# Block-sparse attention and a two-layer MLP on one core: the first weight load moved to the front, a small table moved to GpSimd, and a new order of work

## The chip, the core and the metric

The kernel runs on one core of a Trainium2 chip. Its engines are TensorE (PE: matmuls, with a weight load PEld of its own), VectorE (DVE), ScalarE (ACT), GpSimd (POOL) and SyncE (SP), which here only issues DMA transfers. Each engine works off its own instructions strictly in the order of the program and waits at semaphores for the others; 16 DMA engines move the data. The metric is the time of one execution on the device in microseconds (us), as the median of several runs. The time before is 715.46 us.

## The reference

Two stages. Attention over 4 batches of 8 heads, 768 positions and a head width of 64, with a mask by blocks of 32 positions, and then an MLP over the 3072 x 512 result:

```python
scores = scale * np.matmul(q, k.transpose(0, 1, 3, 2))
mask = np.abs(blk_i - blk_j) <= 1
mask = mask | (blk_i == 0) | (blk_j == 0) | (blk_i == n_blocks - 1) | (blk_j == n_blocks - 1)
for qb in range(n_blocks):
    for kb in sampled_blocks[qb]:           # three sampled blocks for each of the 24
        mask[qb*block:(qb+1)*block, kb*block:(kb+1)*block] = True
scores = np.where(mask, scores, -1000000000.0)
attn = softmax(scores)                      # rows
x = np.matmul(attn, v)                      # -> (3072, 512)
h = x @ w_in                                # 512 x 2048
g = h * np.tanh(softplus(h))
out = g @ w_out                             # 2048 x 512
```

The two weights arrive as 64-bit floats; the other inputs are 32-bit floats, and the sampled blocks are 64-bit integers.

## The kernel before

**Stages.** A block of 32 queries sees its three neighbours, the first and the last block and three sampled ones, eight blocks of keys in all. Queries are worked on two blocks at a time (a *job*, `attend`): scores `s`, row maximum `mx` (VectorE), its negative `nb`, exponentials `pt` (ScalarE), transposes `t` on TensorE and their copies `pp`, the product with v `o`, then on VectorE the normalisation `r`, `xs` (L968 to L983) and a block transpose `tx` (L1001), and a split of the result into two 16-bit parts `xh` and `xl`. The first and the last block of a batch are jobs of their own that see all keys (*dense*). A batch has 13 jobs. Batch 0 is computed in 32 bits (`exact`), the others with split 16-bit parts.

The MLP runs on 256 tokens at a time: `h` (L1206), twelve matmuls for each of 16 column groups, an elementwise chain `hs`, `us`, `g`, and `y` (L1267). The first 256 tokens are blocks 0 to 7 of batch 0; they come from jobs 0 to 4, and job 4 (blocks 7 and 8) is the last that they need.

**Keys and values of the sampled blocks.** Keys are copied from `kt` into the gather buffers `kg` by GpSimd or ScalarE (L691, L693), with offsets read from a table `offk`. Values are gathered by DMA from a padded copy `vd` of v in memory into `vg` (L721 to L727), with row numbers from a table `offv`. Both tables are 72 numbers on one partition, made once at the start by `which` (L362 to L404) from the sampled blocks: duplicates, neighbours and border blocks are sent to a row of zeros.

**Weights.** A weight is 64 bits wide in memory. `w_in` is loaded in eight pieces of 1 MB (`wr`, three buffers, L1051), `w_out` in sixteen pieces of 0.5 MB (`wor`, in the six buffers of the tag `raw`). VectorE unpacks each to 32 bits by three instructions (L1059, L1062, L1065). TensorE then forms weight norms from them (`gram_wi`, `gram_wo`, L468), from which power-of-two scales are made (`rootp`, L494, and `root`, L499 to L352), and ScalarE, VectorE and GpSimd split the scaled weight into two 16-bit parts (`wi t`, `wi hi`, `wi lo` at L1113 to L1124; `wo` at L1156 to L1165).

**What sets the order.** Every step is entered as a task with engines, a modelled duration and what it reads and writes (`Plan.add`). `Plan.emit` goes through them with a clock of its own and gives each engine, in turn, the task that can start first; where several could, the one with the smallest ready time plus an offset from the table `PRIO` (`K(name, n)`). Some tasks may run on one of two or three engines, and the clock chooses. `START` holds the earliest start of the first 18 jobs, in the planner's time. MLP matmuls fill TensorE's queue between attention steps. Where the planner sees TensorE idle in the first 150 us it writes matmuls on zeros in the gap (`zeros`, L1038), whose result nothing uses. DMA transfers of SP are issued in the order of the plan as well; one that waits for a buffer holds those behind it.

## Time and profile before

| | |
|---|---|
| median of 3 runs | 715.46 us (714.55 to 717.31) |
| the profiled execution | 717.17 us |
| its span, first to last instruction | 715.4 us |
| TensorE busy | 679.7 us, 95% |
| VectorE busy | 579.3 us, 81% |
| ScalarE busy | 530.6 us, 74% |
| GpSimd busy | 259.6 us, 36% |
| mean granted TensorE clock | 0.986 |

All rows below come from this one execution. A line such as `L1065` is a line of the kernel before. "Busy" counts the time in which at least one instruction of the engine runs. A row of a timeline gives start, length, engine, line, what is written and read, and in brackets how long the engine stood idle before it and what ended that.

### The profile page before, as it was taken

To read this page: it belongs to the slowest core of one execution; us is meant where nothing else is said; L and a number is where in the kernel's file an instruction comes from. 1 tells how busy PE (TensorE), PEld (TensorE's weight loads), DVE (VectorE), ACT (ScalarE), POOL (GpSimd) and SP (SyncE) were. 2 spreads that over 40 slices of the span, in tenths; PEclk is the share of its full clock that TensorE was granted. 3 is DMA by queue.
4 is the path that set the end of the run, shared out by engine and by line. 5 is a ranking of instruction groups with operands and counts; after the bars stand their busy time and mean duration, and the time that the engine had idled before them with its cause. 6 is when DMAs were issued, how large, how long until landed. Compare 5 with 4: busy or idle time off the path is not lost.

```text
span 715.4 us, 25363 instructions
## 1 busy us (share of the span) xinstructions
PE 679.7 (95%) x10349; PEld 451.6 (63%) x10349; DVE 579.3 (81%) x1083; ACT 530.6 (74%) x874; POOL 259.6 (36%) x326
## 2 busy tenths in 40 slices
...
GB/s 333 383 220 252 269 299 97 124 166 99 173 169 131 199 212 131 163 255 148 143 146 191 137 206 137 245 189 132 162 132 131 134 133 158 131 76 16 16 16 29
DMA packets 144600, 115.94 MB, mean 162 GB/s; under 512 B 96739, under 2 KB 107492, under 8 KB 144484
## 3 DMA queue, kind: packets, MB, share of 16 engines
q1 hardware_dynamic: 144480, 114.33, 60.8%
...
q10 hardware_dynamic: 4, 0.00, 0.0%
...
## 4 chain that ended last, share of the span: by engine, by line
PE 55%; DVE 25%; ACT 7%; DMA 6%; issue 4%; SPq 1%; POOL 1%; ACTq 0%; POOLq 0%; DVEq 0%
PE y L1267 25%; PE h L1206 22%; PE o L947 3%; PE s L777 3%; DVE mx L820 3%; DMA vg<-vd 2%; ACT pt L846 2%; DVE p L897 2%; DVE wi L1065 2%; DMA wr<-in_moe_w_in_dram 1%; DVE wi L1062 1%; DVE tx L1001 1%; DVE hs L1240 1%; DVE nb L835 1%; DVE xs L978 1%
## 5 line engine op out<-in xcount | busy, mean ns | idle before, releaser
L1206 PE MATMUL h<-xh,wi 128*128 128x256 f16 x1536 | 283.1, 273 | 0.0
L1267 PE MATMUL y<-wo,g 128*128 128x512 f16 x1152 | 277.6, 379 | 1.0 <-ACT ys L1278 0.5
L1206 PEld LDWEIGHTS <-wi 128*128 128x128 f16 x2304 | 222.4, 98 | 58.7 <-issue 4.6
L1206 PE MATMUL h<-xl,wi 128*128 128x256 f16 x768 | 209.8, 273 | 0.0
L1267 PEld LDWEIGHTS <-g 128*128 128x128 f16 x1152 | 109.0, 98 | 104.8 <-issue 5.6
L846 ACT ACTIVATE pt<-s,nb,ns 128x256 f32<-128x256 f32 (+1 forms) x208 | 106.4, 577 | 8.2 <-DVE nb L835 7.3
L691 POOL COPY kg<-kt 128x256 f16 (+1 forms) x147 | 77.3, 564 | 75.0 <-PE s L777 54.8
L1215 ACT ACTIVATE hs<-h 128x512 f32<-128x512 f32 x96 | 56.7, 590 | 60.0 <-PE h L1206 59.8
L1240 DVE SCALAR_TENSOR_TENSOR hs<-us,hs 128x1024 f32<-128x1024 f32 x48 | 64.2, 1337 | 28.0 <-ACT us L1239 28.0
L1021 POOL CAST xh<-tx 128x256 f16<-128x256 f32 (+1 forms) x40 | 28.7, 726 | 121.2 <-DVE tx L1001 120.4
L897 DVE SCALAR_TENSOR_TENSOR p<-pt,p 128x512 f16<-128x512 f32 (+1 forms) x102 | 63.6, 643 | 0.8 <-ACT p L890 0.4
L1230 ACT ACTIVATE us<-hs,hsc 128x1024 f32<-128x1024 f32 x48 | 55.2, 1150 | 1.1
L1234 DVE TENSOR_SCALAR us<-us 128x1024 f32<-128x1024 f32 x48 | 34.1, 711 | 26.8 <-ACT us L1230 26.4
L820 DVE TENSOR_REDUCE mx<-s 128x4 f32<-128x1024 f32 x44 | 53.3, 1212 | 3.0 <-PE s L777 2.2
L1251 POOL TENSOR_TENSOR g<-hs,g 128x1024 f16<-128x1024 f32 x18 | 42.4, 2353 | 34.8 <-DVE g L1248 26.0
L1024 POOL TENSOR_TENSOR xl<-tx,xh 128x256 f16<-128x256 f32 (+1 forms) x45 | 37.5, 838 | 41.7 <-ACT xh L1019 25.8
L1238 ACT ACTIVATE us<-us 128x1024 f32<-128x1024 f32 x48 | 50.7, 1057 | 2.3 <-POOL us L1236 1.3
L1237 ACT ACTIVATE us<-us 128x1024 f32<-128x1024 f32 x38 | 40.1, 1055 | 15.7 <-DVE us L1234 15.6
L1239 ACT ACTIVATE us<-us 128x1024 f32<-128x1024 f32 x48 | 50.7, 1057 | 0.8
L693 ACT ACTIVATE kg<-kt 128x256 f16 (+1 forms) x117 | 36.7, 379 | 13.5 <-DMA kt<-in_k_dram 5.4
L947 PEld LDWEIGHTS <-pp 128*32 128x32 f16 x2952 | 32.5, 97 | 11.9 <-issue 11.4
L1253 DVE TENSOR_TENSOR g<-hs,g 128x1024 f16<-128x1024 f32 x30 | 37.4, 1248 | 2.0 <-ACT g L1246 1.6
...
## 6 DMA issues: line engine op xcount, KB each, us to landing
...
```

The lines of the kernel that those rows point to most:

```text
L691: nc.gpsimd.tensor_copy(out=dst, in_=src)
L820: nc.vector.tensor_reduce(out=mx.rearrange("p g w -> p (g w)"), in_=tl[ks].rearrange("p g (w k) -> p (g w) k", k=KT), axis=AX.X, op=ALU.max)
L846: ex = lambda o, x, g, w: nc.scalar.activation(out=o, in_=x, func=AF.Exp, bias=nb[:, g, w:w + 1], scale=ns(w)[:, 0:1])
L897: nc.vector.scalar_tensor_tensor(out=x[:, 1, cs], in0=src, scalar=PSC, in1=x[:, 0, cs], op0=ALU.mult, op1=ALU.subtract)
L947: nc.tensor.matmul(o[cs, at] if v1 == VW else o[cs, at, 0:v1 - v0], p[:, k, g, cs], x, start=j == 0 and g == 0 and k == 0 and n == 0, stop ...
L1206: nc.tensor.matmul(h[:, f2].rearrange("p (s q) -> p s q", q=BS), wi[:, fp, w, cc, fs], x[:, :, cc], start=f2 == 0 and k == 0, stop=f2 == 1 ...
L1215: nc.scalar.activation(out=tl[kq][:, 2 * (fp % 2):2 * (fp % 2) + 2], in_=tl[kh], func=AF.Copy, scale=-2.0 * GSC)
L1230: nc.scalar.activation(out=us(), in_=hs(), func=AF.Exp, scale=hsc[:, b, k:k + 1])
L1238: add("ACT", 0.97, lambda: nc.scalar.activation(out=us(), in_=us(), func=AF.Ln, bias=1.0), w=[ku], key=K("ln", b))
L1239: add("ACT", 0.97, lambda: nc.scalar.activation(out=us(), in_=us(), func=AF.Exp, scale=-1.0), w=[ku], key=K("un", b))
L1240: add("DVE", 1.15, lambda: nc.vector.scalar_tensor_tensor(out=hs(), in0=us(), scalar=-0.5, in1=hs(), op0=ALU.add, op1=ALU.mult), r=[ku], w ...
L1267: nc.tensor.matmul(tl[ky], tl["g", b, t, k][:, g, f, q], wo[:, fc, w], start=fc == 0 and n == 0, stop=fc == NFC - 1 and n == 2)
```

## The change

Three things. The load of the first piece of `w_in` (`load wr` 0) is the first transfer that SP issues; before, the first piece came sixth, behind k, q and v, and it was piece 3. The table of row numbers is taken out of `which` into a task `table` of its own on GpSimd; the not-equal test is written there as a difference or an equality, compared with zero again, which makes 23 instructions of 20, and the rows of zeros are cleared before the loads instead of after the table. And the numbers that set the order (`PRIO`, `START`, `RES`) are all new.

```diff
 PRIO = {
-    "load wr": (163.9, 188, 32.3, -243.6, 177.7, 103.9, 211.3, 300.2),
+    "load wr": (-961.5, -388, 51.1, -141.9, 314.6, 167.6, 315, 492.8),
+    "table": (-1252,),
...
     def which(new):
         room = new(sb, "hs", ("z",), [P, 4, TT]).rearrange("p c t -> p (c t)")
+        tl["z"] = room[0:BS, 0:H * VW // 2]
+        nc.gpsimd.memset(tl["z"], 0.0)
...
         nc.scalar.dma_start(out=kq, in_=blocks[0:1])
+        tl["kq"] = kq, sbi, mk
+
+    def table():
+        kq, sbi, mk = tl["kq"]
         qb = mk(NB)
-        nc.vector.tensor_copy(out=qb.rearrange("p (c g) -> p c g", g=GPC), in_=kq[:, :, 0:GPC])
+        nc.gpsimd.tensor_copy(out=qb.rearrange("p (c g) -> p c g", g=GPC), in_=kq[:, :, 0:GPC])
...
-        nc.vector.tensor_tensor(out=ar, in0=ar, in1=ar, op=ALU.mult)
-        nc.vector.tensor_scalar(out=ar, in0=ar, scalar1=1.5, scalar2=None, op0=ALU.is_gt)
+        nc.gpsimd.tensor_tensor(out=ar, in0=ar, in1=ar, op=ALU.mult)
+        nc.gpsimd.tensor_scalar(out=ar, in0=ar, scalar1=1.5, scalar2=None, op0=ALU.is_gt)
         for j in (0, NB - 1):
-            nc.vector.tensor_scalar(out=nq, in0=rb, scalar1=float(j), scalar2=None, op0=ALU.not_equal)
-            nc.vector.tensor_tensor(out=ar, in0=ar, in1=nq, op=ALU.mult)
+            nc.gpsimd.tensor_scalar(out=nq, in0=rb, scalar1=float(j), scalar2=0.0, op0=ALU.is_equal, op1=ALU.is_equal)
+            nc.gpsimd.tensor_tensor(out=ar, in0=ar, in1=nq, op=ALU.mult)
...
-    add("ACT", 1.0, lambda: which(new), w=["off", "z"],
-        new=[("hs", ("z",))], key=K("which", 0), lat=5.2, kind=("dma", 0.0, 2))
+    add("ACT", 1.0, lambda: which(new), w=["kq", "z"],
+        new=[("hs", ("z",))], key=K("which", 0), lat=3.6, kind=("dma", 0.0, 2))
+    add("POOL", 6.0, table, r=["kq"], w=["off"], use=[("z",)], key=K("table", 0))
...
-    RES, START = 949.9, [53.9, 10.3, 0, 62.9, 42.9, 3.5, 60.8, 74.5, 31.2, 92.3, 3.1, 0, 64.4, 30.3, 104.4, 183, 166.3, 159.2]
+    RES, START = 2183, [1, 0, 36, 10.2, 0, 5.1, 56.9, 31.3, 89.8, 28.4, 117.5, 0, 0, 122, 149.1, 139.3, 196.9, 34.9]
```

The sync queue (SP) at the start of the program, before; `wr` is a piece of `w_in`, `kt`, `q` and `raw_v` are the loads of k, q and v of batch 0, `vd` is the padded copy of v:

```order
L519 DMA kt_124<-in_k_dram 128x4x768
L519 DMA q_0_154<-in_q_dram 128x4x256
L537 DMA raw_v_0_158<-in_v_dram 128x2x512
L519 DMA q_1_160<-in_q_dram 128x4x256
L537 DMA raw_v_1_162<-in_v_dram 128x2x512
L1051 DMA wr_164<-in_moe_w_in_dram 128x4x512
L537 DMA raw_v_2_166<-in_v_dram 128x2x512
L407 DMA vd_63<-z 32x1040
L1051 DMA wr_191<-in_moe_w_in_dram 128x4x512
```

And now, at the same place:

```order
L1057 DMA wr_124<-in_moe_w_in_dram 128x4x512
L525 DMA kt_134<-in_k_dram 128x4x768
L525 DMA q_0_138<-in_q_dram 128x4x256
L543 DMA raw_v_0_140<-in_v_dram 128x2x512
L1057 DMA wr_142<-in_moe_w_in_dram 128x4x512
L543 DMA raw_v_1_144<-in_v_dram 128x2x512
L1057 DMA wr_146<-in_moe_w_in_dram 128x4x512
L413 DMA vd_63<-z 32x1040
```

Three pieces of the weight stand among the first seven transfers instead of one; the second load of q has moved behind the fourth piece.

VectorE around the first unpacking, before; `offv` is the last row of the table, `mx` the maximum of the dense job 0 and then of job 1:

```order
L400 TENSOR_TENSOR z<-z 1x72
L401 TENSOR_SCALAR offv<-z 1x72
L635 COPY v_0_150<-raw_v_0_158 128x16x64
L815 TENSOR_REDUCE mx_240<-s_214 128x2
L817 TENSOR_REDUCE mx_240<-s_0_0_223 128x1
L817 TENSOR_REDUCE mx_240<-s_0_1_224 128x1
L818 TENSOR_TENSOR mx_240<-mx_240 128x2
L1059 TENSOR_SCALAR wi<-wr_164 128x1024
L1062 SCALAR_TENSOR_TENSOR wi<-wr_164,wi 128x1024
L1065 SCALAR_TENSOR_TENSOR wi<-wr_164,wi 128x1024
L820 TENSOR_REDUCE mx_344<-s_284 128x4
```

And now, from the engine's first instruction:

```order
L1065 TENSOR_SCALAR wi<-wr_124 128x1024
L1068 SCALAR_TENSOR_TENSOR wi<-wr_124,wi 128x1024
L1071 SCALAR_TENSOR_TENSOR wi<-wr_124,wi 128x1024
L641 COPY v_0_130<-raw_v_0_140 128x16x64
L821 TENSOR_REDUCE mx_261<-s_224 128x2
L823 TENSOR_REDUCE mx_261<-s_0_0_233 128x1
L823 TENSOR_REDUCE mx_261<-s_0_1_234 128x1
L824 TENSOR_TENSOR mx_261<-mx_261 128x2
L1065 TENSOR_SCALAR wi<-wr_142 128x1024
L1068 SCALAR_TENSOR_TENSOR wi<-wr_142,wi 128x1024
L1071 SCALAR_TENSOR_TENSOR wi<-wr_142,wi 128x1024
L826 TENSOR_REDUCE mx_360<-s_301 128x4
```

The table has left VectorE, one unpacking stands in front of everything, and a second one is done by the maximum of job 1.

VectorE ahead of the normalisation of job 4, before (`o_1296` is that job's output, `wor` a piece of `w_out`, `iv_i` and `ws` the scale of a quarter of `w_in`, `gsc` made of all four):

```order
L1062 SCALAR_TENSOR_TENSOR wo<-wor_1262,wo 128x512
L499 TENSOR_SCALAR iv_i<-tp_w_1227 128x1
L502 TENSOR_SCALAR iv_i<-iv_i 128x1
L352 TENSOR_SCALAR ws_1426<-iv_i 128x1
L1065 SCALAR_TENSOR_TENSOR wo<-wor_1262,wo 128x512
L1062 SCALAR_TENSOR_TENSOR wo<-wor_1005,wo 128x512
L1180 TENSOR_SCALAR hsc<-iv_i,iv_x 128x1
L1065 SCALAR_TENSOR_TENSOR wo<-wor_1005,wo 128x512
L1171 TENSOR_REDUCE gmx<-iv_i 128x1
L1173 RECIPROCAL rg<-gmx 128x1
L1174 TENSOR_SCALAR gsc<-iv_i,rg 128x4
L968 TENSOR_SCALAR r_1467<-o_1296,iv_r 128x4
```

And now, where job 4's output is `o_1435` and job 3's `o_1309`:

```order
L1068 SCALAR_TENSOR_TENSOR wo<-wor_1326,wo 128x512
L974 TENSOR_SCALAR r_1425<-o_1309,iv_r 128x4
L978 RECIPROCAL r_1425<-r_1425 128x4
L989 TENSOR_TENSOR xs_1428<-o_1309,r_1425 128x256
L1071 SCALAR_TENSOR_TENSOR wo<-wor_1326,wo 128x512
L1007 STREAM_TRANSPOSE tx_1454<-xs_1428 128x256
L826 TENSOR_REDUCE mx_1462<-s_1237 128x4
L885 COPY pp_1_1501<-t_1_1392 128x512
L974 TENSOR_SCALAR r_1512<-o_1435,iv_r 128x4
L978 RECIPROCAL r_1512<-r_1512 128x4
L989 TENSOR_TENSOR xs_1515<-o_1435,r_1512 128x256
L505 TENSOR_SCALAR iv_i<-tp_w_1506 128x1
```

Before, eight pieces of `w_out` are unpacked and all four scales of `w_in` made ahead of that row; now fourteen pieces are unpacked ahead of it (the last is `wor_1326`), and two of the four scales follow behind it.

## Rows read from the trace of the kernel before

**Rows 1.** The page: busy time, share of the span and instructions of each engine.

```profile
PE 679.7 (95%) x10349; PEld 451.6 (63%) x10349; DVE 579.3 (81%) x1083; ACT 530.6 (74%) x874; POOL 259.6 (36%) x326
```

**Rows 2.** Stretches: length, busy (instructions) of PE, PEld, DVE, ACT, POOL; clock, DMA, GB/s.

```profile
0.00:89.76 89.76, 71.52 (x1241) 42.19 (x1241) 76.55 (x139) 50.88 (x104) 46.03 (x63) 0.92 0.91 291
89.76:160.00 70.24, 63.71 (x1087) 48.21 (x1080) 67.52 (x119) 58.31 (x93) 41.99 (x49) 0.95 0.62 174
160.00:700.00 540.00, 533.31 (x7996) 356.36 (x7978) 435.21 (x827) 420.05 (x676) 171.57 (x216) 1.00 0.59 143
```

**Rows 3.** The same for the filler line L1038 alone (PE and PEld busy).

```profile
0.00:89.76 89.76, 32.36 (x119) 11.81 (x119) 0.92 0.91 291
```

**Rows 4.** Timeline of TensorE: the dense scores, and around the first MLP matmul.

```profile
9.00 1.52 PE L767 MATMUL s<-kt,q 64*32 64x512 f32 x32 [1.57 <-DMA q<-in_q_dram]
...
79.44 0.55 PE L931 MATMUL o<-vg,pp 128*32 128x65 f32 x24 [1.36 <-DMA vg<-vd]
79.93 0.40 PE L468 MATMUL gram_wo<-wo 128*128 128x128 bf16 x4
80.17 1.31 PE L1038 MATMUL zeros<-z 128*128 128x512 f16 x3
...
89.76 0.28 PE L1206 MATMUL h<-xh,wi 128*128 128x256 f16 x1
```

**Rows 5.** Timeline of VectorE, from the last piece of the first weight on.

```profile
57.23 3.04 DVE L1065 SCALAR_TENSOR_TENSOR wi<-wr,wi 128x1024 int32<-128x1024 int32 x1
...
83.08 0.21 DVE L968 TENSOR_SCALAR r<-o,iv_r 128x4 f32<-128x4 f32 x1
...
83.88 1.21 DVE L820 TENSOR_REDUCE mx<-s 128x4 f32<-128x1024 f32 x1
...
92.14 0.68 DVE L1065 SCALAR_TENSOR_TENSOR wo<-wor,wo 128x512 int32<-128x512 int32 x1
92.74 0.68 DVE L1062 SCALAR_TENSOR_TENSOR wo<-wor,wo 128x512 int32<-128x512 int32 x1
93.34 0.41 DVE L1059 TENSOR_SCALAR wo<-wor 128x512 int32<-128x512 int32 x1
```

**Rows 6.** Timeline of VectorE at the start: table, copy of v, first unpacking.

```profile
5.31 0.17 DVE L380 COPY z<-z 1x24 f32<-1x24 f32 x1 [5.31 <-DMA z<-in_blocks_dram]
...
9.64 0.18 DVE L401 TENSOR_SCALAR offv<-z 1x72 int32<-1x72 f32 x1
10.25 0.69 DVE L635 COPY v<-raw_v 128x1024 f32<-128x1024 f32 x1 [0.42 <-DMA raw_v<-in_v_dram]
...
15.55 0.69 DVE L1059 TENSOR_SCALAR wi<-wr 128x1024 int32<-128x1024 int32 x1 [2.62 <-DMA wr<-in_moe_w_in_dram]
...
17.58 1.23 DVE L1065 SCALAR_TENSOR_TENSOR wi<-wr,wi 128x1024 int32<-128x1024 int32 x1
```

**Rows 7.** Timeline of GpSimd: copies from k, a small and a long subtraction.

```profile
7.42 0.74 POOL L653 COPY kg<-kt 128x256 f32<-128x256 f32 x2 [5.18 <-DMA kt<-in_k_dram]
8.54 0.77 POOL L691 COPY kg<-kt 128x128 f32 x3 [0.38 <-issue]
...
16.63 3.27 POOL L691 COPY kg<-kt 128x128 f32 x6 [2.48 <-ACT pt L846]
...
29.31 0.43 POOL L1024 TENSOR_TENSOR xl<-tx,xh 128x128 f16<-128x128 f32 x1
...
56.08 3.12 POOL L1123 TENSOR_TENSOR wi<-wt_i,wi 128x1024 f16<-128x1024 f32 x1
```

**Rows 8.** Timeline of the sync queue: the issues of k and the first weight piece.

```profile
0.75 0.46 SPq L519 DMA_DIRECT2D kt<-in_k_dram  x1
...
4.82 0.68 SPq L1051 DMA_DIRECT2D wr<-in_moe_w_in_dram  x1
```

**Rows 9.** Waits of TensorE from 90 us on: total us, times, longest.

```profile
PE gram_wo L468 <- DVE wo L1065: 2.4, 3, 1.2
```

**Rows 10.** Waits of the sync queue up to 60 us: total us, times, longest.

```profile
SPq L1051 <- DVE wi L1065: 5.8, 4, 2.5
```

161 lines of the change are left out of this document (80 added, 81 removed), and 30 rows, old and new, of the table PRIO.

## The prediction

> **What bounds the kernel now.** I read the busy shares of the page first: TensorE is busy 679.7 of 715.4 us [rows 1]. The number flatters, because a part of that is no work. The table by stretches [rows 2] and the same table for the filler line alone [rows 3] split the span at 89.76 us, where the first matmul of the MLP starts [rows 4]. Up to there TensorE is busy 71.5 us, of which 32.4 us are 119 filler matmuls on zeros (0.272 us each). So the first 89.76 us hold 39.1 us of real work and 18.2 + 32.4 = 50.6 us that give nothing. Behind it TensorE loses 6.5 us up to 160 and 6.7 us up to 700; the 4.2 us that are left of the span are its tail. Check: 679.7 - 32.4 = 647.3 us of real work, and 647.3 + 50.6 + 6.5 + 6.7 + 4.2 = 715.3. The order of work does not touch the 647.3; the change can win or lose only in the four losses, and the first is the large one. It is set by one event: when the output of attention job 4 (blocks 7 and 8, the last that the first 256 tokens need) is normalised, transposed and split, since the first MLP matmul reads it.
>
> What holds that event is read in two views. VectorE is busy 76.6 of these 89.8 us [rows 2], and 5.3 + 0.4 + 2.6 of the 13.2 it lacks lie before the first unpacking at 15.55 [rows 6]; from there on it works off a queue whose bulk is the unpacking of the weights, and comes to the normalisation of job 4 (L968) at 83.08 [rows 5]. The DMA engines are busy 91% of the same stretch [rows 2], and the last gather of job 4 lands only at 79.44, with TensorE waiting 1.36 us for it [rows 4]. Two limits lie close together, VectorE the later one.
>
> **The change, part by part.** *The table.* 20 VectorE instructions from 5.31 to 9.82 go (4.5 us) [rows 6]. They lie where VectorE had only loads to wait for: the copy of v at 10.25 and the first weight piece at 15.55 both come on a DMA. Taken out alone they are worth nothing there; the stretch is only free for something else. On GpSimd 23 instructions take their place. The trace of before has no such small arithmetic on GpSimd; the nearest row is a 128x128 subtraction of 0.43 us [rows 7], and the lower end is VectorE's own pitch of 0.23. That makes 5.3 to 9.9 us. While VectorE unpacked, GpSimd's copies took 3.27 us for six against 0.77 for three, twice as long [rows 7], and the first unpacking will run just then, so I take 8 us, from 5.3 to 13.3. The first copies from k into the gather buffers follow (0.74 and 0.77 us [rows 7]) and are wanted when the scores of job 1 start, behind the exponentials of job 0, by my estimate near 18 us. The cover is some 3 us; beyond it each us of the table delays job 1.
> The Trainium skill (GPSIMD Engine Reference, section Key points) says that VectorE is about twice as fast for elementwise work; twice the 4.5 us would be 9 us, inside the bounds and hidden as well.
>
> *The first piece in front.* Before, k (1.57 MB) is issued at 0.75 and the first weight piece (1.05 MB) at 4.82 [rows 8]; the copies that need k start at 7.42 [rows 7] and the unpacking at 15.55 [rows 6]. From the one landing to the other came the piece and 2.1 MB of q and v, 3.1 MB in 8.1 us or 0.39 MB/us. The piece at the head then lands 1.3 us before k did, near 6, and k, q and v come 2.7 us later: the dense scores of job 0 start near 11.7 instead of 9.00 [rows 4]. VectorE unpacks the piece (15.55 to 18.81, 3.2 us [rows 6]) in the hole that the table left, so at 15.5 us it is 3.2 us ahead. The pieces share three buffers, so the next loads are issued earlier too. What attention loses is 2.7 us at its start; the same VectorE queue takes it in.
>
> *The order.* In front of job 4's normalisation stand 14 pieces of the second weight, unpacked, against 8. A piece is three instructions with steps of 0.60, 0.60 and at most 0.41 us [rows 5]: 1.6 us, so +9.6; one more maximum, +1.2 [rows 5]; one small subtraction, +0.2. Behind it went two roots of weight scales with what hangs on them and the three steps up to gsc, thirteen tiny instructions at VectorE's pitch of about 0.2: -2.6. The splitting of the first weight's rear half stands behind too, so GpSimd has 4 of its long subtractions in front instead of 7. Each holds VectorE: L1065 took 3.04 us while one ran from 56.08 to 59.20, against 1.23 [rows 5 to 7]. Three fewer are worth 3 x 1.8 = 5.4 at most and nothing at least; I take 3.5. With the 3.2 us in hand: 9.6 + 1.2 + 0.2 - 2.6 - 3.5 - 3.2 = +1.7, so VectorE comes to job 4 at 84.8 (82.9 to 88.3).
> The DMA limit: in front of job 4's last gather the sync queue now has 6 more pieces of 0.52 MB and one gather fewer (0.46 MB), 2.7 MB, 7.0 us at 0.39. The 9% that DMA stood free up to 79.4, 7 us, can take all of it or none: landing at 79.4 to 86.4, plus 0.7 for the matmuls. I take 85 for the normalisation, VectorE being the later one again.
> From there to the first MLP matmul it was 6.7 us, with a maximum of 1.2 in between and two subtractions on VectorE. Now come the normalisation and one root (six tiny instructions, 1.4), the transpose (0.6), and casts on ScalarE and subtractions on GpSimd (two each of at most 0.43 [rows 7]): 3.7 in all. First MLP matmul at 88.7 (86.6 to 93). Before it TensorE has done one job's P.V less (two of 0.55 x 32/24 = 0.73 us) and 40 of the weight-norm matmuls more (four start 0.24 us ahead of the next row [rows 4]: 2.4), 0.9 us net. The first loss is thus 88.7 - 40.0 = 48.7, **1.9 us less**. The program carries 111 fillers instead of 119, 8 x 0.272 = 2.2 us; that is no proof, since TensorE may idle where no filler stands.
> Behind 88.7: TensorE waited 2.4 us for unpacked pieces of the second weight [rows 9]; 14 of 16 are now done by then. **-2** (0 to -2.4). From 160 on the order is set anew but of the same kind: as many changes between attention and MLP (213 in either program), and of the 39 score groups no two closer than before. Its 6.7 us of loss can become 3 to 10; I take **0**.
> Sum: -1.9 - 2 = -3.9. The profiled execution took 717.17 us for its span of 715.4; the sum gives 713.3 for one like it. The median of the runs is 715.46, 1.7 below it, and so I forecast **711.5**.
>
> **The rivals.**
> *Loads first, gathers late (slower).* The gathers of jobs 3 and 4 stand on the sync queue behind six loads in a row, which wait for buffers; up to 60 us the queue already waits 5.8 us in four such places, 2.5 the longest [rows 10]. If DMA does not run denser than its 291 GB/s [rows 2], 2.7 MB cost 9.3 us: the gather lands at 88.7, the first MLP matmul comes at 88.7 + 0.7 + 3.7 = 93.1, the loss is 53.1, +2.5; with one more such wait of 2.5 us ahead of each of the two jobs +7.5, less the 2: 721. It decides from a first MLP matmul later than about 95. For it: DMA 91% busy. Against: the free 9% were waits for buffers, and these now turn earlier.
> *Nothing is won (same).* The earlier unpacking only moves VectorE's idle time, because attention starts 2.7 us late and the table stretches beside it: VectorE comes to job 4 at 84.8 + 2.7, the MLP at 91.2, loss 51.2, 0.6 more, and half of the 2 us behind it comes: 715.1.
> *The late losses go too (much faster).* If the new order also halves the 6.5 and 6.7 us, another 4 to 5 us: 707. Nothing in the rows speaks for it but that they are waits, not work.
> *GpSimd stops at an operation that is new to it.* Its first subtraction in the trace (29.31) starts in a row of work and takes 0.43 us [rows 7], so the rows speak against it. As a mechanism of this kernel: a table 6 us longer ends at 19.3, the copies for job 1 at 20.8, some 3 us past the cover: 714.5.
> The Trainium skill (GPSIMD Engine Reference, section Instruction dispatch) has such a stop of about 6 us, for the first call of a freshly loaded kernel, without a row of its own in a profile; by that this rival holds, by the rows it does not.
>
> **How the numbers follow.** About 0.5% (3.6 us) is what can be told from no change, so 711.9 is the border. Forecast 0.50, its own range 707 to 715, with 0.30 of it under the border and 0.20 over; late gathers 0.17; nothing won 0.15; late losses gone 0.13; GpSimd's stop 0.05. Faster 0.30 + 0.13 = 0.43; same 0.20 + 0.15 + 0.03 = 0.38; slower 0.17 + 0.02 = 0.19. The range leaves half of the late gathers and a part of the late losses outside: 704.5 to 719.5.
>
> **What would show it.** Right: the first unpacking starts near 6 us and the dense scores near 11.7; the table's 23 rows end before 15; VectorE is at job 4's normalisation near 85, behind 14 pieces; the first MLP matmul comes at 87 to 90, with TensorE's busy time less fillers near 40 us by then; no waits for unpacking behind it; a loss from 160 to 700 of 3 to 10 us. Wrong: a first MLP matmul past 92, TensorE waiting for the gathers of jobs 3 and 4 in rows of 2 us and more, the scores of job 1 waiting for the copies from k, or a loss from 160 on that differs by over 4 us, which would say that the order and not the start decides.

## The result, and the profile after

The changed kernel takes **724.83 us** (median of 4 runs, 724.24 to 725.85) against 715.0 us of the kernel before on the same chip: 1.0134 times the time, 95% interval 1.0107 to 1.0162. It is slower by some 9.8 us where 4 us less were forecast, and lies outside the range. The profiled execution took 725.06 us for a span of 723.3; that of the kernel before (717.17 us, span 715.4) lay above its median, so the two spans differ by 7.9 us only. Line numbers behind line 409 are 6 higher than before.

The table by stretches, which answers to [rows 2], now split at 93.0 where the MLP starts; the columns are the stretch, its length, the busy time of PE, PEld, DVE, ACT and POOL with instructions, PEclk, DMA share and GB/s:

```profile
0.00:93.00 93.00, 72.17 (x1210) 44.04 (x1211) 75.08 (x131) 44.20 (x101) 41.03 (x75) 0.89 0.90 301
93.00:160.00 67.00, 58.03 (x1002) 44.08 (x999) 59.08 (x100) 58.40 (x95) 47.34 (x45) 0.92 0.48 132
160.00:700.00 540.00, 530.96 (x8046) 355.70 (x8045) 437.50 (x840) 419.59 (x670) 175.75 (x226) 1.00 0.61 145
```

And the filler line alone in the first stretch (PE, PEld, PEclk, DMA share, GB/s), which answers to [rows 3]:

```profile
0.00:93.00 93.00, 29.23 (x111) 10.67 (x111) 0.89 0.90 301
```

The reader is to take four numbers out of these for each kernel: when the MLP starts, what real work is left for TensorE from there on, what it loses up to 160 and up to 700, and the tail. Their sum is the span.

| | before | after | forecast |
|---|---|---|---|
| first MLP matmul | 89.76 | 93.0 | 88.7 |
| real work behind it | 608.2 | 608.3 | 607.3 |
| loss up to 160 | 6.5 | 9.0 | 4.5 |
| loss from 160 to 700 | 6.7 | 9.0 | 6.7 |
| tail | 4.2 | 4.0 | 4.2 |
| span | 715.4 | 723.3 | 711.4 |

The 7.9 us of span are 3.2 of a later start of the MLP, 2.5 behind it and 2.3 from 160 on. Against the forecast the span is 11.9 us longer: 4.3 by the start of the MLP, 4.5 behind it, 2.3 from 160 on and 1.0 of real work. The first loss as the prediction counted it (idle and fillers ahead of the MLP) is 50.1 instead of 50.6, so by that number nothing is lost there. That number misleads: TensorE's real work ahead of the MLP has grown from 39.2 to 42.9 us. Of that 0.9 had been forecast, as matmuls that the new order moves ahead; the rest goes with the granted clock of the stretch, 0.89 instead of 0.92. The clock's lower level is half the upper, so 0.11 of 93 us are 20.5 us at the lower level, where before had 14.

The start, on VectorE, answers to [rows 6] (start, length, line, what is done, and the idle time before it):

```profile
9.74 0.70 DVE L1065 TENSOR_SCALAR wi<-wr 128x1024 int32<-128x1024 int32 x1 [9.74 <-DMA wr<-in_moe_w_in_dram]
10.47 1.22 DVE L1068 SCALAR_TENSOR_TENSOR wi<-wr,wi 128x1024 int32<-128x1024 int32 x1
11.73 1.23 DVE L1071 SCALAR_TENSOR_TENSOR wi<-wr,wi 128x1024 int32<-128x1024 int32 x1
16.32 0.69 DVE L641 COPY v<-raw_v 128x1024 f32<-128x1024 f32 x1 [3.36 <-DMA raw_v<-in_v_dram]
17.33 1.23 DVE L821 TENSOR_REDUCE mx<-s 128x2 f32<-128x1024 f32 x1 [0.31 <-PE s L773]
...
23.41 1.23 DVE L826 TENSOR_REDUCE mx<-s 128x4 f32<-128x1024 f32 x1 [0.15 <-PE s L773]
...
89.50 0.21 DVE L974 TENSOR_SCALAR r<-o,iv_r 128x4 f32<-128x4 f32 x1
```

VectorE stands idle for 9.74 us until the piece at the head has landed, and comes to the first maximum at 17.33. Before, it came to it at 10.86:

```profile
10.86 1.22 DVE L815 TENSOR_REDUCE mx<-s 128x2 f32<-128x1024 f32 x1
```

On TensorE, in the same time and behind the first MLP matmul, which answers to [rows 4]:

```profile
13.02 1.03 PE L474 MATMUL gram_wi<-wi 128*128 128x128 bf16 x8 [5.90 <-DVE wi L1071]
...
15.26 2.76 PE L773 MATMUL s<-kt,q 64*32 64x512 f32 x32
...
92.97 0.27 PE L1212 MATMUL h<-xh,wi 128*128 128x256 f16 x1
...
98.98 0.87 PE L937 MATMUL o<-vg,pp 128*32 128x65 f32 x32 [3.23 <-DMA vg<-vd]
...
133.34 0.67 PE L937 MATMUL o<-vg,pp 128*32 128x65 f32 x32 [3.25 <-issue]
```

The dense scores start at 15.26, 6.3 us later than before, and run for 2.76 us instead of 1.52: TensorE has been idle for 5.9 us and is at the lower clock level. The last two rows are the larger part of the loss behind the first MLP matmul, two waits of 3.2 us each that the kernel before does not have.

### The profile page after: what moved, and what is told of

The parts are those of the page before. It is cut to its first block, busy times and chain, and to the rows that moved or that the text cites. A ratio compares the mean times of both kernels' runs of the same rounds, so it can differ in the third digit from the quotient of the medians.

```text
span 723.3 us, 25320 instructions
## 1 busy us (share of the span) xinstructions
PE 680.5 (94%) x10341; PEld 452.4 (63%) x10341; DVE 574.8 (79%) x1073; ACT 526.7 (73%) x869; POOL 264.1 (37%) x344
## 4 chain that ended last, share of the span: by engine, by line
PE 57%; DVE 22%; ACT 8%; DMA 6%; issue 4%; SPq 1%; POOL 1%; ACTq 0%; DVEq 0%; POOLq 0%
PE y L1273 24%; PE h L1212 23%; PE o L953 3%; PE s L783 3%; DMA wor<-in_moe_w_out_dram 3%; DVE p L903 2%; DVE mx L826 2%; ACT pt L852 2%; DVE hs L1246 2%; DMA vg<-vd 2%; DVE xs L984 1%; DMA wr<-in_moe_w_in_dram 1%; DVE us L1240 1%; PE o L937 1%; PE s L773 1%
## 5 line engine op out<-in xcount | busy, mean ns | idle before, releaser
L697 POOL COPY kg<-kt 128x256 f16 (+1 forms) x141 | 68.4, 523 | 80.2 <-PE s L783 62.8
L1246 DVE SCALAR_TENSOR_TENSOR hs<-us,hs 128x1024 f32<-128x1024 f32 x48 | 61.5, 1281 | 31.5 <-ACT us L1245 31.5
L1027 POOL CAST xh<-tx 128x256 f16<-128x256 f32 (+1 forms) x41 | 26.2, 648 | 131.4 <-DVE tx L1007 130.6
L1244 ACT ACTIVATE us<-us 128x1024 f32<-128x1024 f32 x48 | 50.5, 1055 | 4.5 <-POOL us L1242 3.8
L1245 ACT ACTIVATE us<-us 128x1024 f32<-128x1024 f32 x48 | 50.7, 1056 | 0.7
L1257 POOL TENSOR_TENSOR g<-hs,g 128x1024 f16<-128x1024 f32 x15 | 35.5, 2368 | 32.7 <-ACT g L1252 24.7
L1243 ACT ACTIVATE us<-us 128x1024 f32<-128x1024 f32 x33 | 34.8, 1054 | 14.1 <-DVE us L1240 14.0
L1242 POOL TENSOR_TENSOR us<-us 128x1024 f32<-128x1024 f32 x15 | 31.9, 2130 | 35.1 <-DVE us L1240 32.1
## 6 DMA issues: line engine op xcount, KB each, us to landing
wr<-in_moe_w_in_dram SPq DMA_DIRECT2D x8, 1024.0 KB, 11.9
```

The source lines that it names most:

```text
L697: nc.gpsimd.tensor_copy(out=dst, in_=src)
L1244: add("ACT", 0.97, lambda: nc.scalar.activation(out=us(), in_=us(), func=AF.Ln, bias=1.0), w=[ku], key=K("ln", b))
L1245: add("ACT", 0.97, lambda: nc.scalar.activation(out=us(), in_=us(), func=AF.Exp, scale=-1.0), w=[ku], key=K("un", b))
L1246: add("DVE", 1.15, lambda: nc.vector.scalar_tensor_tensor(out=hs(), in0=us(), scalar=-0.5, in1=hs(), op0=ALU.add, op1=ALU.mult), r=[ku], w ...
```

## The experiments

Sixteen kernels were run. Each was compared with runs of the kernel before on its own chip, so ratios are compared here, not medians. Names that begin with b_ are edits of the kernel before, with a_ of the changed one. Where the text says that the **order is held**, the planner has gone through as always, but its list of steps is executed afterwards, with a few of them moved; every other step keeps its place, its engine and its fillers. `ahead(s, a, b)` puts step a ahead of step b in that list, `behind` behind it; `m`, `first` and `last` count steps of one name. The third entry of a step is the number of fillers ahead of it, and `step(k)` is the place of the k-th MLP step on TensorE. The changed kernel ran on one chip only, and none of the runs repeats it on another chip with its order held and nothing moved; how far its ratio differs from chip to chip is not known.

| kernel | ratio to before (95%) | first MLP matmul | span of the profiled run |
|---|---|---|---|
| the changed kernel | 1.0134 (1.0107 to 1.0162) | 93.0 | 723.3 |
| b_table | 0.9997 (0.9972 to 1.0021) | 90.5 | 715.2 |
| b_head | 1.0089 (1.0062 to 1.0117) | 94.8 | 722.5 |
| b_both | 1.0081 (1.0052 to 1.0109) | 92.9 | 717.7 |
| a_start | 1.0100 (1.0076 to 1.0124) | 91.6 | 720.1 |
| a_start2 | 1.0084 (1.0055 to 1.0114) | 94.9 | 723.2 |
| b_mid | 1.0021 (0.9997 to 1.0044) | 91.5 | 716.4 |
| a_gath | 1.0184 (1.0143 to 1.0224) | 93.4 | 728.7 |
| a_fill | 1.0080 (1.0056 to 1.0103) | 94.9 | 724.6 |
| b_fill | 1.0053 (1.0024 to 1.0083) | 92.3 | 721.1 |
| a_late | 1.0072 (1.0044 to 1.0100) | 93.5 | 717.6 |
| a_late_fill | 1.0085 (1.0051 to 1.0119) | 94.3 | 717.9 |
| a_all | 1.0055 (1.0023 to 1.0088) | 95.0 | 717.1 |
| b_late | 1.0008 (0.9992 to 1.0024) | 89.6 | 718.9 |

x_w, x_v and a_wo have one execution each, and the stretch that they were made for is what counts in them. A profile shows one execution, and not always a typical one: that of b_both is the fastest of its four, that of a_fill the slowest of its five.

### The parts in the old order: b_table, b_head, b_both

b_table moves the table alone; every step keeps its place:

```diff
-        nc.vector.tensor_tensor(out=ar, in0=ar, in1=ar, op=ALU.mult)
+        nc.gpsimd.tensor_tensor(out=ar, in0=ar, in1=ar, op=ALU.mult)
...
```

> The kernel before with every instruction in its place, only the 20 table instructions moved from VectorE to GpSimd (23 there, with the rows of zeros cleared ahead). Theory 'start' (what the first 15 us lose is carried to the end): VectorE's table lay in a hole that stays a hole, GpSimd's ends near 12 instead of 9.8, so the copies for job 0 and 1 come some 2 us later than before but still ahead of job 1's scores: 715 to 716. Theory 'order' (the loss comes from waits that the new numbers place behind 40 us): 715, no change. Both say that the table is not where 9.8 us came from; above 718 both are wrong on it.

No change, 0.9997. The table ends at 14.25 on GpSimd, later than expected, and costs nothing all the same: it is not where the time went.

b_head moves one load:

```diff
+    ahead(s, ("load wr", 3), ("load32 k", 0))
```

> The kernel before with every instruction in its place, only the load of the first weight piece (piece 3) moved from the sixth to the first place of the sync queue. k then lands near 13.7 as in the changed kernel, the dense scores start there instead of at 9.0, VectorE comes to its first maximum near 15.5 instead of 10.9 and to the first unpacking near 18 instead of 15.5. Theory 'start': VectorE's queue up to job 4 shifts by 2.5 to 5 us and the first MLP matmul with it, 718 to 721. Theory 'order': the DMA engines and the buffers hold that event anyway, the shift is taken in by what VectorE stood idle (13 us), 715 to 717.

1.0089. The two rows that matter, the dense scores on TensorE and the first maximum on VectorE:

```profile
14.92 2.81 PE L796 MATMUL s<-kt,q 64*32 64x512 f32 x32 [6.97 <-DMA q<-in_q_dram]
```

```profile
16.98 1.23 DVE L844 TENSOR_REDUCE mx<-s 128x2 f32<-128x1024 f32 x1
```

Scores 5.9 us late, the first maximum 6.1 us late, the first MLP matmul 5.1 us late (94.84 against 89.76 [rows 4]), and the time 0.9% longer. What the start loses is carried to the end; VectorE's idle time does not take it in. Not all of the 5.1 us need be the start's, though: TensorE also stops for 2.18 us in the midst of a group of matmuls (up to 61.68) with nothing awaited that the profile shows, and b_both, with the same late start and no such stop, has its first MLP matmul 3.1 us late.

b_both adds what was meant to pay for it, the early unpacking, and the table on GpSimd:

```diff
+    ahead(s, ("load wr", 3), ("load32 k", 0))
+    for m in range(3):
+        ahead(s, ("decode wr", 3), ("copy v", 0), m)
```

> The kernel before with the two named parts of the change and its old order: table on GpSimd, first piece at the head of the sync queue, and its unpacking put first on VectorE (ahead of the first copy of v); all else in its place. The unpacking runs from 9.7 to 13, before k has landed, so VectorE has 3.2 us in hand against the head load alone. Theory 'start': 716 to 719, the rest of the 9.8 us being the order's. Theory 'order': 714 to 716, the start being worth nothing in either direction.

1.0081: the unpacking starts at 9.21 and is done before k has come, the first maximum is at 17.14, and the time is no better than with the load alone, by the intervals. In the old order the named part of the change costs 0.8% (0.5 to 1.1), more than either theory gave it but for the lower end of the interval.

### What a load at the head costs: x_w and x_v

The kernel before with one more load of 1.05 MB ahead of k, which nothing reads; once rows of the weight, once rows of v:

```diff
+            if what == "k":
+                room = wi[:, 6:8].rearrange("p k t c f -> p (k t c f)").bitcast(I32)
+                nc.sync.dma_start(out=room.rearrange("p (c f) -> p c f", c=NCC), in_=w_in.rearrange("(p c) f -> p c f", p=P)[:, :, 0:4 * P])
```

```diff
...
+                nc.sync.dma_start(out=room.rearrange("p (c f) -> p c f", c=NCC), in_=v[1, 0:4 * P].rearrange("(c p) d -> p c d", p=P).bitcast(I32))
```

> The kernel before in its old order, with one more load ahead of k: 1.05 MB of the first weight, in the form of a weight piece (128 partitions x 4 rows of 2 KB, the rows 16 KB apart in memory), into room that is free until the pieces 6 and 7 are unpacked; nothing reads it. It asks what a load at the head costs k and q. Theory 'bytes': 1.05 MB at 0.39 MB/us, the dense scores start 2.7 us late, at 11.7. Theory 'weight rows': a weight piece takes some 9 us to land whatever else is on the way and what is behind it lands late with it, the scores start near 15. Theory 'first in line': whatever stands first pays a start of its own, then this run and the next are both near 15.

> The same as the run with the weight rows ahead of k, but the 1.05 MB are rows of v (128 partitions x 4 rows of 2 KB, rows of neighbouring partitions 2 KB apart in memory). Theory 'bytes': scores at 11.7. Theory 'weight rows': scores at 11.7 here and near 15 there. Theory 'first in line': near 15 in both.

The dense scores and the landing of the extra load (in us from its issue), with the weight's rows:

```profile
14.83 2.82 PE L770 MATMUL s<-kt,q 64*32 64x512 f32 x32 [7.24 <-DMA q<-in_q_dram]
```

```profile
L521 SPq DMA_DIRECT2D wi<-in_moe_w_in_dram x1: 699/699/699, 0.8 to 0.8; - x1
...
DMA to landing us min/median/max: 8.5/8.5/8.5
```

and with rows of v:

```profile
12.18 2.82 PE L770 MATMUL s<-kt,q 64*32 64x512 f32 x32 [4.67 <-DMA q<-in_q_dram]
```

```profile
L521 SPq DMA_DIRECT2D wi<-in_v_dram x1: 461/461/461, 0.8 to 0.8; - x1
...
DMA to landing us min/median/max: 5.9/5.9/5.9
```

The same bytes cost k and q 3.2 us as rows of v and 5.8 us as rows of the weight. The forecast's 2.7 us was near the price of bytes; the other 2.6 us come with the weight. Its rows lie 16 KB apart in memory and those of v 2 KB, but the tensor changed along with the distance, so which of the two makes the difference is not shown. In the trace of the changed kernel 491 of the piece's 512 rows have been started by 6.0 us, when the whole piece was forecast to have landed, and the last 21 only from 6.0 to 9.1, most of them 0.25 to 0.36 us long where 0.084 is usual for a row of 2 KB; VectorE's wait ends with the last of them. k's rows behind them have their usual length of 0.121 us, but the last of them starts at 13.0 instead of 6.8.
The Trainium skill (DMA: Bandwidth & Descriptors, section "Why a DMA increments its semaphore by 16 and not by 1") says that a transfer runs on up to 16 engines that finish independently and counts as landed with the last one. The 21 late rows agree with that.

### The start put back in the new order: a_start, a_start2

```diff
+    behind(s, ("load wr", 0), ("load v", 0))
+    behind(s, ("gram wi", 0), ("s", 0), last=0)
```

> The changed kernel with its new order, but its start put back: table on VectorE, the load of the first piece behind k, the first q and the first v, and the weight-norm matmuls of that piece behind the dense scores. Scores of job 0 then start near 9 instead of 15.3. Theory 'start': the first MLP matmul comes 3 to 5 us earlier and the time is 716 to 720. Theory 'order': DMA and the gathers hold that event and the later waits stay (3.2 us at 99, 3.3 at 130, 2.4 more from 160 on): 722 to 725.

1.0100, but the run does not test what it was made for: on VectorE the unpacking still stood ahead of the first maximum, waited for the piece until 13.15, and the maximum came at 16.88. So the start was put back on every engine (the table is on VectorE in both):

```diff
+    behind(s, ("load wr", 0), ("load v", 0))
+    s[where(s, "gram wi", 0)][2], s[where(s, "s", 0)][2] = 0, 20
+    behind(s, ("gram wi", 0), ("s", 0), last=0)
+    ahead(s, ("copy v", 0), ("decode wr", 0))
+    ahead(s, ("s", 0), ("copy v", 0))
+    behind(s, ("mx", 0), ("copy v", 0))
```

> The changed kernel with its new order from the first maximum on, and its start really put back on every engine: table on VectorE, the first piece's load behind k, the first q and the first v; on TensorE fillers, then the dense scores, then the weight-norm matmuls of that piece; on VectorE the copy of v, the first maximum, then the unpacking. In the run with the start put back in part VectorE still stood at the first piece until 13.15 and came to the first maximum at 16.88, as in the changed kernel. Now the first maximum is at 10.9 and the unpacking at 13.2. Theory 'start is carried to the end' (as the old order showed with the head load, 6.1 us later at the maximum and 6.4 at the end): 717 to 719. Theory 'the new order loses by itself, behind 40 us': 721 to 724.

The first maximum on VectorE, and the first MLP matmul:

```profile
10.81 1.20 DVE L855 TENSOR_REDUCE mx<-s 128x2 f32<-128x1024 f32 x1
```

```profile
94.90 0.27 PE L1246 MATMUL h<-xh,wi 128*128 128x256 f16 x1
```

6.5 us earlier at the maximum, and 1.9 us later at the MLP. But the lead is gone long before, at the second maximum, and by the edit itself:

```profile
16.25 1.03 PE L508 MATMUL gram_wi<-wi 128*128 128x128 bf16 x8 [5.83 <-DVE wi L1105]
17.08 5.44 PE L1078 MATMUL zeros<-z 128*128 128x512 f16 x19
22.45 0.40 PE L807 MATMUL s<-kt,q 64*32 64x96 f32 x16
```

```profile
23.70 1.23 DVE L860 TENSOR_REDUCE mx<-s 128x4 f32<-128x1024 f32 x1 [3.67 <-PE s L807]
```

On TensorE the scores of job 1 stand behind the norm matmuls, which wait 5.83 us for the unpacking, and behind 19 fillers. They start at 22.45, and VectorE, which waits 3.67 us for them, is at the second maximum at 23.70 instead of 23.41. So this run does not price an early start in the new order either. What it shows is that the kernel stays 0.84% slower with none of the named parts of the change and with the start lost in another way. Set beside the 0.81% of b_both that makes 1.65% against 1.34% together; with intervals of 0.3 on each, whether the two add up stays open, and so does whether the 0.5% from 1.0134 to 1.0084 is a gain (the intervals just touch).

### What of the new order costs it: a_wo, a_gath, a_late

a_wo puts the order numbers of the second weight back, and everything is ordered anew:

```diff
-    "load wo": (-385.3, -129.2, -918.4, 1118),
-    "decode wor": (-539.6, -106.7, -453.3, -290.4),
-    "gram wo": (-1009,),
+    "load wo": (5.1, 39.8, -463.1, 534.1,),
+    "decode wor": (-599.6, 24.8, -199.8, -61.5,),
+    "gram wo": (-838.3,),
```

> The changed kernel with the order numbers of the second weight alone put back to those of before (its loads, unpacking and norm matmuls); everything is ordered anew from that, and by the order 7 pieces of it stand ahead of job 4's normalisation on VectorE instead of 14. Only the first MLP matmul is looked at, since the rest of the order changes as well. It tells apart why putting the start back did not help (first MLP matmul at 94.9 with the first maximum at 10.8). Theory 'second weight first': its loads fill the sync queue and the DMA engines ahead of the gathers of jobs 2 to 4, and TensorE's norm matmuls and VectorE's unpacking stand ahead of those jobs; without half of them the first MLP matmul comes at 85 to 89. Theory 'late start': the weight's place does not matter, 92 to 94.

The MLP starts at 90.40, 2.6 us earlier, not the 4 to 8 us that were expected. Everything else was ordered anew with it, so that the weight's place is the cause is not shown. The one execution took 738.06 us, 2.8% above the kernel before on its chip: TensorE loses 16.7 us from 160 to 700 in that order, at places that the three rows of numbers do not name.

In a_gath three loads of k and two pieces of the second weight stand behind the gathers of job 5. In the changed kernel they stand ahead (start, length, line, transfer on the sync queue):

```profile
85.62 1.50 SPq L543 DMA_DIRECT2D raw_k<-in_k_dram  x3
87.21 1.04 SPq L1057 DMA_DIRECT2D wor<-in_moe_w_out_dram  x2
88.34 0.39 SPq L727 DMA_DIRECT2D vg<-vd  x1
89.63 1.43 SPq L733 DMA_DIRECT2D vg<-vd  x3
```

The last rows of the gather that begins at 88.34 are issued from 89.63 on and land 8.8 us later, where such transfers (L733) take 1.9 us in the median, and TensorE waits for them until 98.98.

```diff
+    behind(s, ("gather v", 9), ("gather v", 8))
+    behind(s, ("load k", 3), ("gather v", 9))
+    for _ in range(2):
+        behind(s, ("load wo", 3), ("load k", 3), m=2, last=0)
```

> The changed kernel, its order held, with one move on the sync queue: the three loads of the next batch's k and two pieces of the second weight (2.6 MB) stand behind the two gathers of job 5 instead of ahead of them. In the changed kernel TensorE waits 3.2 us for that gather at 99 (issued at 88.3, landed 8 us later), two MLP steps after the MLP began, and the clock is at its lower level from 100 to 105. Theory 'gathers late behind loads': the wait falls under 1 us and the time by 2 to 4 us, 720 to 723. Theory 'moved only': the norms of k, now later, hold ScalarE and the MLP's own chain as long: 723.5 to 726.

```profile
108.14 0.61 PE L506 MATMUL gram_wo<-wo 128*128 128x128 bf16 x4 [11.32 <-DVE wo L1103]
```

1.0184, worse. The wait for the gather is gone, and a wait of 11.3 us has taken its place: the two pieces of the weight are now issued behind everything else, VectorE waits for one of them for 10.5 us, and TensorE's norm matmuls for them stand in line ahead of everything else. A wait was not removed but moved, and it grew.

a_late leaves the transfers alone and moves what waits. Job 5's P.V matmuls get two more MLP steps ahead of them. For the wait at 133.34, which the trace puts down to nothing it shows ("issue"), VectorE's rows tell the cause:

```profile
129.96 1.21 DVE L821 TENSOR_REDUCE mx<-s 128x2 f32<-128x1024 f32 x1
...
132.36 0.21 DVE L974 TENSOR_SCALAR r<-o,iv_r 128x4 f32<-128x4 f32 x1
132.60 0.18 DVE L978 RECIPROCAL r<-r 128x4 f32<-128x4 f32 x1
132.82 0.42 DVE L989 TENSOR_TENSOR xs<-o,r 128x256 f32<-128x256 f32 x1
```

The normalisation of job 8 (132.36 to 133.24) frees the one buffer into which job 9's P.V product goes, and it stands behind the maximum of another job. In a_late it stands ahead of it:

```diff
+    ahead(s, ("hs", 0), ("ss k", 3), first=2)
+    for k in (2, 3):
+        s.insert(where(s, "o", 0, 11), s.pop(step(k)))
+    behind(s, ("mx", 0), ("xs", 0), m=10, last=8)
+    behind(s, ("nb", 0), ("mx", 0), m=10, last=10)
```

> The changed kernel, its order held but for two places behind the first MLP matmul. At 99 the P.V matmuls of job 5 stand behind four MLP steps instead of two (and ScalarE's first copy of the MLP's output ahead of the last of three norms of k), so that TensorE works while the gather lands. At 133 VectorE normalises job 8 ahead of the maximum of the dense job 10, instead of behind it: the P.V matmuls of job 9 at 133.34 wait for that normalisation (132.4 to 133.2), since there is one buffer for that product. Theory 'two late waits': both go but for some 1 us together, and the lower clock behind them with them: 5.5 us less of waits and up to 4 of stretched work, 717 to 721. Theory 'given back': the next steps wait as long, 723 to 725.

```profile
98.78 0.66 PE L971 MATMUL o<-vg,pp 128*32 128x65 f32 x32
```

```profile
127.28 0.67 PE L971 MATMUL o<-vg,pp 128*32 128x65 f32 x32 [0.84 <-PE h L1246]
```

```profile
93.45:160.00 66.55, 59.29 (x1057) 44.38 (x1055) 61.97 (x105) 60.01 (x96) 48.23 (x49) 1.00 0.53 142
```

Job 5's product starts at 98.78 as ever, but TensorE has worked up to there; job 9's starts at 127.28 behind a wait of 0.84. The loss to 160 falls from 9.0 to 7.3 and the clock of the stretch rises from 0.92 to 1.00. The time goes from 1.0134 to 1.0072: some 0.6%, 4.4 us, for moves at two places. That these moves win time is shown, by intervals that lie apart (though the two ratios come from two chips); how much of it is the two waits themselves is less clear. Of the 5.7 us between the two spans 1.7 are waits and 1.4 TensorE's work behind the first MLP matmul, which takes 606.9 us instead of 608.3 with the clock up; 0.5 go the other way at the start of the MLP, and 3.0 come from 160 on, where nothing was moved.

### What the lower clock costs: a_fill, a_late_fill, b_fill

More fillers at places where TensorE stood idle, all else held:

```diff
+    for name, n, m, more in (
+        ("gram wi", 0, 0, 24), ("t", 0, 7, 6), ("o", 0, 3, 9), ("gram wo", 0, 0, 8), ("o", 0, 9, 5),
+        ("o", 0, 11, 12), ("gram wo", 0, 14, 3)):
+        s[where(s, name, n, m)][2] += more
```

> The changed kernel, its order held, with 67 more fillers on TensorE at seven places where it stood idle up to 101 us (24 ahead of the weight-norm matmuls at 13.0, 12 ahead of the wait at 99, 3 to 9 at the others). It prices the lower clock: TensorE's own work is 651.2 us in the changed kernel and 647.4 before, with 30 us at the lower level against 20. Theory 'clock': the stretches at 10 to 20, 40 to 45, 50 to 55 and 100 to 106 come back to the full level, the work shrinks by 2.5 to 4 us and the time by about as much: 720.5 to 722.5. Theory 'cover': up to 93 TensorE's work is not on the path, so only the stretch behind 99 counts, 2 us: 722.5 to 723.5. Theory 'no': the fillers run over and cost what they give: 724 to 726.

1.0080, some 0.5% better than the changed kernel, but by a way that its profile, of the slowest execution, does not show: the MLP starts at 94.9, later. a_late_fill has the first five of these on top of a_late:

> The same as the run with the two late places moved, with 52 more fillers at five places ahead of the first MLP matmul (24 ahead of the norm matmuls at 13). Theory 'they add up': the fillers alone took the kernel from 1.34% above before to 0.8%, so 2 to 4 us less than the run without them, 714 to 718. Theory 'one cause': the fillers gave only what the late place at 99 now gives, the same time as the run without them.

1.0085 against 1.0072: no gain from the fillers once the late places are moved. The mean clock up to the MLP is 0.97 instead of 0.87, TensorE's work there is 39.5 us instead of 44.3, and what it loses by waiting and fillers is 54.8 instead of 49.2. That looks as if the stretched work ahead of the MLP lay beside waits for others and cost nothing, but another thing hides what the clock gives back. Just ahead of the first MLP matmul TensorE stops in the midst of one group of score matmuls, with nothing awaited that the profile shows ("issue"), here in a_late_fill and then in a_all (below):

```profile
92.40 0.39 PE L810 MATMUL s<-kt,q 64*32 64x96 f32 x5 [2.13 <-issue]
```

```profile
94.18 0.43 PE L816 MATMUL s<-kg,q 64*32 64x160 f32 x2 [2.58 <-issue]
```

a_fill has a stop of 1.90 us at the same place, the changed kernel and a_late have none there. In each of the three a 16 KB transfer on the instruction queue ended 1.4 to 1.5 us before the engine went on. That TensorE waited for its own instructions is argued from that and was not tried. Without the stop the MLP of a_late_fill would start near 92.2 (an estimate: 94.32 less 2.13), ahead of the 93.45 of a_late, so what the lower clock costs is not priced by these runs. b_fill does the same in the kernel before, at eleven places:

```diff
+        ("s", 0, 0, 5), ("rootp w", 1, 0, 6), ("gram wi", 0, 0, 4), ("rootp w", 2, 0, 2), ("o", 0, 6, 3),
+        ("gram wi", 3, 1, 7), ("t", 0, 11, 3), ("t", 0, 13, 4), ("gram wo", 0, 5, 2), ("gram wo", 0, 7, 4), ("o", 0, 13, 3)):
```

> The kernel before, its order held, with 44 more fillers at eleven places where TensorE stood idle for 0.8 to 1.9 us up to 100 us and mostly fell to the lower clock behind (28 to 34, 60 to 68, 100 to 105). Theory 'clock': 20 us at the lower level become some 10, the work shrinks by 1 to 2 us from 100 us on and the path to the first MLP matmul by up to 1: 712.5 to 714.5. Theory 'cover': 714.5 to 716. Theory 'no' (fillers end behind the event waited for): 716 to 718.

1.0053, slower, with the mean clock at 0.994 instead of 0.986, and the MLP starts 2.6 us later. TensorE stops twice in the same way ahead of it, for 2.27 us (up to 29.32) and 1.84 (up to 66.03), where the kernel before has no such stop; whether the stops come of the fillers, and whether the fillers also end behind what was waited for, as one theory said, is not shown. Either way this kernel became slower.

### Everything put back, and two attempts on the kernel before

a_all is a_late with the start of a_start2 (the norm matmuls of the first piece behind the scores of job 1) and 32 fillers:

> The changed kernel with the late places moved, 32 fillers, and its start put back (table on VectorE, the first piece's load behind k, the first q and v, its norm matmuls behind the scores of job 1, its unpacking behind the first maximum). What is left of the change is the rest of the new order. Theory 'three causes': start 0.3 to 0.5%, late waits and clock together 0.8%: 713 to 716, the time of before. Theory 'the order's other places': what it loses from 40 to 93 and from 160 on stays, 718 to 721.

1.0055, in the range of the second theory: start, late places and fillers together give back 0.8 of the 1.34%, and beyond a_late (1.0072) no gain is clear of the intervals. Here the start does come through, at first: VectorE is at the second maximum at 20.00 instead of 23.41. At job 4's normalisation (88.58) 0.9 us of the 3.4 are left, since VectorE now waits 3.2 us for pieces of the second weight where it waited 1.6, and the stop of 2.58 us shown above puts the first MLP matmul at 95.0 all the same. The 0.55% that are left belong to other places of the new order or to what the fillers bring with them; these runs do not name them.

b_mid and b_late look for a kernel faster than before:

```diff
+    behind(s, ("load wr", 3), ("load32 q", 0))
+    behind(s, ("copy v", 0), ("mx", 0), last=0)
```

> The kernel before with two steps moved: the load of its first weight piece stands third on the sync queue, right behind k and the first q (before: sixth), and the first copy of v stands behind the first maximum on VectorE. The dense scores stay at 9.0, the piece lands near 13 instead of 15.5, as VectorE ends the first maximum at 12.9, so VectorE is 2 to 2.6 us ahead from there on. Theory 'VectorE's queue up to job 4 sets the end': 712.5 to 714.5. Theory 'DMA and the gathers set it': 714.5 to 716.5. It could lose if v, landing later, holds the store that the gathers read.

1.0021, no gain. The unpacking starts at 13.87, 1.7 us earlier than before, but the scores of job 1 at 18.70, 3 us later, behind job 0's exponentials; the time of one is spent on the other.

```diff
+    s.insert(where(s, "gram wo", 0, 4), s.pop(step(1)))
+    for k in (2, 3):
+        s.insert(where(s, "gram wo", 0, 5), s.pop(step(k)))
+    s.insert(where(s, "gram wo", 0, 7), s.pop(step(4)))
+    ahead(s, ("pp", 0), ("mx", 0), m=21, first=11)
+    ahead(s, ("pp", 0), ("nb", 0), m=22, first=11)
```

> The kernel before, its order held but for a few places behind its first MLP matmul. TensorE: the norm matmuls of the second weight that wait for unpacked pieces at 91.7, 94.4 and 98.6 (0.42, 0.80 and 1.16 us) stand behind the next MLP steps instead of ahead of them. VectorE: two copies of transposed probabilities for the dense job 10, for which TensorE waits at 136.3 and 138.6 (0.83 and 1.05 us), stand ahead of a maximum and of two small steps. Theory 'late places': 2 to 3.5 us less, the lower clock at 100 to 104 may go as well, 712 to 714 where before is 715. Theory 'given back': the unpacking sets the end of the norm matmuls anyway and the next step waits, within 1 us of before. It would lose if the norms of the second weight, now later, hold back the first product with it.

TensorE's waits from 90 to 160 us (who waits for whom: us in all, times, longest):

```profile
PE o L966 <- DVE pp L914: 1.8, 2, 1.0
PE o L966 <- DMA vg<-vd: 1.7, 1, 1.7
PE gram_wo L503 <- DVE wo L1100: 1.3, 1, 1.3
```

1.0008: given back. The norm matmuls wait 1.3 us instead of 2.4 [rows 9], but a gather is now waited for 1.7 us, and the two copies are waited for as long as they were. No kernel tried here beats the one before.

## Why the prediction was wrong, step by step

**What bounds the kernel.** Right in its main line: TensorE's work behind the first MLP matmul is the same in both kernels (608.2 and 608.3), and the time is set by when the MLP starts and what is lost behind it. Wrong in one point: "the order of work does not touch the 647.3". It is 651.2 now, with the mean clock at 0.979 instead of 0.986. That the 3.7 us more ahead of the MLP are covered by waits is likely, since VectorE comes last there (below), but not shown: the runs with fillers have stops that hide it.

**The table.** Hidden, as forecast (b_table). But its 23 rows take 10.7 us, from 4.18 to 14.89, above the upper bound of 9.9, here the first and last of them and the slow ones in the middle:

```profile
4.18 0.20 POOL L387 COPY z<-z 1x24 f32<-1x24 f32 x1 [1.94 <-DMA z<-in_blocks_dram]
...
9.95 0.66 POOL L404 TENSOR_SCALAR z<-z 1x24 f32<-1x24 f32 x1
10.69 1.12 POOL L406 TENSOR_TENSOR z<-z 1x24 f32<-1x24 f32 x1
11.89 1.16 POOL L403 TENSOR_TENSOR z<-z 1x24 f32<-1x24 f32 x1
...
14.49 0.40 POOL L409 TENSOR_SCALAR offv<-z 1x72 int32<-1x72 f32 x1
```

The rows of 0.25 us become 1.1 while VectorE's two-input unpacking runs (10.47 to 12.96). In b_both, where it runs from 9.94 to 12.42, two rows that start then take 1.15 and 1.26 us; in b_table, where VectorE does not unpack beside the table, the same rows take 0.22 and 0.30.
The Trainium skill (GPSIMD Engine Reference, section Key points) says that GpSimd shares its SBUF interfaces with VectorE and contends with instructions that have two SBUF inputs there; the rows agree, with a factor of four on these.

**The first piece in front: the step that failed first.** Forecast: the piece lands near 6, k, q and v come 2.7 us later. Measured: 9.74 and 6 us. The price was taken from a rate between two landings, 0.39 MB/us. The page of the kernel before had the answer in another place, the list of DMA issues (the last number is the median time from issue to landing):

```profile
wr<-in_moe_w_in_dram SPq DMA_DIRECT2D x8, 1024.0 KB, 10.6
...
raw_v<-in_v_dram SPq DMA_DIRECT2D x12, 512.0 KB, 4.9
```

A piece of this weight takes 10.6 us from its issue in the median; at the head of an idle queue it took 9.0. x_v and x_w split the price of 5.8 us: 3.2 for the bytes, 2.6 more for rows of the weight. And "the same VectorE queue takes it in" is refuted by b_head: 6.1 us at the first maximum became 5.1 at the first MLP matmul and 0.9% of the time. Nor was VectorE ahead by the unpacking's 3.2 us. It did unpack ahead of the first maximum, but 3.7 us after the forecast, and was through with both at 19.4, where the kernel before had done the same at 18.8 [rows 6]: 0.6 us behind instead of 3.2 ahead.

**The order, up to the MLP.** VectorE comes to job 4's normalisation at 89.50, forecast 84.8 to 85; from there to the MLP it took 3.5 us, forecast 3.7. The count of 14 pieces ahead held. Of the 4.7 us that the forecast missed here, 3.8 are the term "3.2 us in hand", which measured 0.6 the other way: with it put right, the forecast's own sum gives 83.1 + 9.6 + 1.2 + 0.2 - 2.6 - 3.5 + 0.6 = 88.6, 0.9 short of what was measured. So the failed price of the load is also the failed step here, and that VectorE's queue sets the event held in this kernel:

```profile
78.69 0.32 PE L937 MATMUL o<-vg,pp 128*32 128x65 f32 x8 [0.70 <-DMA vg<-vd]
79.33 0.88 PE L937 MATMUL o<-vg,pp 128*32 128x65 f32 x24 [0.32 <-DMA vg<-vd]
...
86.83 0.67 PE L937 MATMUL o<-vg,pp 128*32 128x65 f32 x32 [1.36 <-DVE xs L989]
87.77 0.66 PE L937 MATMUL o<-vg,pp 128*32 128x65 f32 x32
```

TensorE waits 1.0 us for job 3's gather and not at all for job 4's; job 4's P.V waits 1.36 us for VectorE to normalise job 3. This is read from one trace; a run that gives back the start alone in this order, with nothing else lost, was not made. The second limit is close behind: in a_all 2.5 us of a lead of 3.4 went, mostly into waits for pieces of the second weight.

**Behind the MLP: -2 forecast, +2.5 measured.** The waits for unpacked pieces of the second weight did shrink, from 2.4 us to 1.0. Two waits of 3.2 us came in their place, one for a gather behind five loads, one for a normalisation behind another job's maximum. The forecast took a wait removed for time won and did not ask what stands next in line on an engine that works strictly in order; the order of the steps, which stands before any run, had both places. Moving what stands there won 0.6% (a_late).

**From 160 on: 0 forecast, +2.3 measured**, inside the bounds of 3 to 10. In the runs this loss lies between 4.2 and 9.2 us in kernels whose steps there are in the same places as in their parent (4.2 in a_all, 6.0 in a_late, 9.0 in the changed kernel; 5.4 in b_table, 6.7 before, 9.2 in b_fill). So it does not depend on its own steps alone; what else sets it was not tried.

**The rivals.** "Loads first, gathers late" had the sign, and its 93.1 for the first MLP matmul (measured 93.0) is luck: its path, a late gather of job 4, did not occur. Its mechanism came at another place, at the gather of job 5, behind the start of the MLP, which was waited for 3.2 us behind five loads. It was given 0.17; with the landing times of the page it should have had more. "Nothing is won" put the MLP at 91.2. "The late losses go too" had the wrong sign. "GpSimd stops at an operation that is new to it" falls: the 23 rows follow one another with gaps of under 0.1 us.

**What the prediction named as signs of being wrong** came true in one point, a first MLP matmul past 92. TensorE did wait for gathers in rows of 2 us and more (2.31 at 51, 3.23 at 99), but not for those of jobs 3 and 4, as the sign had it: these are of job 1 and job 5. The scores of job 1 did not wait for the copies from k, and the loss from 160 on differs by 2.3 us, not by over 4.
